# Four tokens per partition for the later query loads, one activation table set for Ln and Exp, and new instruction orders, in a fused linear-attention and feed-forward kernel

## The chip, the cores and the metric

The kernel runs on one core of a Trainium2 chip. The metric is the device time of one execution in microseconds, as the median of several runs. A core has five engines with a queue each: TensorE (PE, with its weight loads as PEld), VectorE (DVE), ScalarE (ACT), GpSimd (POOL) and SyncE (SP), which here only issues transfers. Sixteen DMA engines move the data.

## The reference

Two functions run one after the other: a decaying linear attention and a feed-forward layer with a sine.

```python
def _attn_ref(q, k, v, lam):            # q, k, v: (4, 8, 768, 64)
    pos = np.arange(64); rel = pos[:, None] - pos[None, :]
    Dmask = np.where(rel >= 0, lam[:, None, None] ** rel, 0.0)
    for b in range(12):
        sl = slice(64 * b, 64 * b + 64)
        qb, kb, vb = q[:, :, sl], k[:, :, sl], v[:, :, sl]
        intra = (qb kb^T * Dmask) vb
        out[:, :, sl] = intra + (qb * lam ** (pos + 1)) kv_state
        kv_state = lam ** 64 * kv_state + (kb * lam ** (63 - pos))^T vb

def _moe_ref(x, w_in, w_out, alpha):    # x: (3072, 512), d_ff = 2048
    h = x @ w_in
    s = np.sin(alpha * h)
    g = h + s * s / (alpha + 1e-9)
    return g @ w_out
```

The products above are written in words; `x` is the attention's output with the eight heads side by side. Inputs and output are 32-bit floats.

## The kernel before

**Tiling.** Attention works on 24 blocks of 128 tokens, six for each of the four batch entries (`NB` = 6). Instead of a decay mask, query and key are scaled by powers of lambda (tables `Lq`, `Lk`, `Lp`, `Lq4`, made from `exp(n ln lambda)` in the prologue), so that a 0/1 mask is left. For each block, `scale_block` multiplies the loaded 32-bit `q32` and `k32` by their table into the bf16 tile `qk2` and casts `v32` into `v2`. `piece_Q`, `piece_K` and `piece_T` transpose `qk2` into `qkT`, on TensorE for the first eight blocks, by a transposing transfer issued from SP for the rest. `part_S` makes the score products, which VectorE multiplies by the mask into `Sm` (L629); `part_O` adds the masked scores times `v2` and the queries times the running state; `part_Z` accumulates the state in one bank, from which `Zd` or `Zc` is evicted. The attention result of a block is evicted transposed into `xT` (L732, and L745 for the first four blocks).

**Feed-forward.** Six chunks of 512 tokens. `unit_A` and `unit_A2` (L828, L862) multiply `w1` by `xT`; ScalarE takes the sine (`t16`), ScalarE or POOL squares it (`u16`), VectorE adds it to the product as `gT` (L845, L880), which frees the bank. `unit_B` (L893) is the second product for chunk 0. From chunk 1 on the second product is done with seven half-size products instead of eight (`unit_P`, L981): `weight_sums` (L936) and `token_sums` (L959) form the sums that this needs, and `finish` combines the seven terms through `kept` (L1018, L1021, L1027) before the stores. `store` (L913) puts the stores of chunk 0 on ScalarE's queue.

**Order.** Every operation is recorded by `_Plan.op` with what it reads and writes. The order on each engine, and for operations that several engines can do also the engine, is written out by hand as lists of operation numbers in `_Plan.ORDER` (L38 to L103). `_settle` walks these lists; `emit` puts a semaphore wait before each operation whose input comes from elsewhere. Each queue runs strictly in its list's order. A pair `(n, cols)` in TensorE's list is a filler: n products of `cols` columns on constant data, which keep TensorE busy in the prologue.

**The prologue.** The loads of the first four blocks go out on SP, 3 MB in runs of 1,024 bytes (`load_q(0)`: four tokens of a head in each partition). ScalarE takes `Ln` of lambda (L438), then a first `Exp` (L440, a table load), VectorE multiplies by the exponents (`lnL`, L441), ScalarE takes the four tables (L443 to L449) and loads the table for the sine (L450). Then come scalings, transposes, scores and masks for four blocks, and the first unit of the feed-forward (L862).

**The later query loads.** For each pair of blocks s, s + 1 from 4 on, `load_q` issues one load of 512 KB: partition p holds tokens 2p and 2p + 1 of all eight heads, in runs of 512 bytes. So the queries of a pair come out of the transposes split by token parity, and `queries(s)` gives for a block two runs of 64 columns, one of each parity. Scores and results then have their 128 query columns in the order (parity, index); the mask of these blocks (`mask[2]`) is made for it, and the eviction to `xT` puts them back in order, writing every second bf16 element.

## Time and profile before

| | us |
|---|---|
| three runs | 210.6, 210.4, 210.04 |
| median | 210.4 |
| the profiled execution | 209.95 |
| its span, first to last instruction | 208.2 |
| mean granted TensorE clock | 1.000 |

A row of the timeline is start, length, engine, line, operation, output and inputs, and in brackets the idle time before it with what ended it. A row of the groups is line, engine, operation, names, shapes and count, then the busy time in all and the mean in ns of one, then the idle time before. Rows of the waits are total, times, longest. `PEld` overlaps `PE`. `SPq`, `ACTq` and `POOLq` are the engines' own queues while they issue a transfer. The span also shows 34.40 MB moved at 165 GB/s on average, 83,222 packets, 59,632 of them under 512 bytes.

### The profile page before, as it was taken

Reading aid. Unit: us, or ns where it says so; the run is one execution under the profiler, and the core shown is the slowest. Engines: PE = TensorE matmul, PEld = TensorE weight load, DVE = VectorE, ACT = ScalarE, POOL = GpSimd, SP = SyncE. Lnnn points to the kernel's source line nnn. Section 1 sums busy time; section 2 is a strip of 40 time slices with the busy share of each in tenths; the row PEclk is TensorE's granted clock in tenths of the full one; section 3 lists DMA queues with packets and bytes.
Section 4 is the critical chain, followed back from the end, with each engine's and each line's share of the span. In section 5 each row is a group of like instructions: output and inputs, shape, how many; then the busy total and the mean of one; then the engine's idle time right before and its main releaser. Section 6 shows DMA issues by size and latency. Waiting matters only on the chain.

```text
span 208.2 us, 4897 instructions
## 1 busy us (share of the span) xinstructions
PE 200.0 (96%) x1972; PEld 136.8 (66%) x1972; DVE 168.5 (81%) x296; ACT 147.7 (71%) x270; POOL 132.4 (64%) x140
## 2 busy tenths in 40 slices
PE   6988999999997999998999999999999999999995
PEld 6756444557765877665657576665667666667994
DVE  2898567886989999987988979899798866767854
ACT  5658999448998999976979776898765579734300
POOL 6065689834968987954796850958851695585400
DMA  4999999999899999799997999380300004000324
GB/s 133 323 315 216 202 255 214 213 238 245 197 179 230 232 250 248 154 215 206 208 245 156 242 271 185 67 194 26 136 0 3 0 32 169 3 0 20 128 94 165
DMA packets 83222, 34.40 MB, mean 165 GB/s; under 512 B 59632, under 2 KB 80384, under 8 KB 83200
## 3 DMA queue, kind: packets, MB, share of 16 engines
q1 hardware_dynamic: 78544, 29.24, 62.5%
q0 software_dynamic: 3696, 3.67, 10.9%
q10 hardware_dynamic: 960, 1.19, 1.9%
q8 instruction: 15, 0.25, 0.5%
q14 instruction: 7, 0.06, 0.1%
HBM read 27.28 MB, written 6.29 MB: 161 GB/s over the span
## 4 chain that ended last, share of the span: by engine, by line
PE 79%; DVE 9%; ACT 4%; DMA 3%; SPq 2%; issue 1%; ACTq 1%; POOL 0%
PE bank L828 28%; PE bank L981 26%; PE bank L862 7%; PE bank L893 6%; PE bank L722 3%; PE bank L618 3%; DMA v<-in_v_dram 3%; SPq L324 2%; DVE gT L880 2%; DVE Sm L629 2%; DVE gT L845 2%; PE bank L700 1%; DVE w L936 1%; PE bank L654 1%; ACT Zd L672 1%; PE bank L662 1%
## 5 line engine op out<-in xcount | busy, mean ns | idle before, releaser
L828 PE MATMUL bank<-xT,w 128*128 128x512 bf16 x296 | 70.9, 380 | 1.0 <-ACT kept L1018 0.7
L845 DVE SCALAR_TENSOR_TENSOR gT<-u,rinv,bank 128x512 bf16<-128x512 bf16 x74 | 53.6, 744 | 18.2 <-ACT u L842 14.1
L838 ACT ACTIVATE t<-bank,alpha 128x512 bf16<-128x512 f32 x74 | 49.9, 683 | 19.9 <-PE bank L828 19.0
L828 PEld LDWEIGHTS bank<-xT,w 128*128 128x128 bf16 x296 | 27.8, 98 | 28.8 <-DVE gT L845 1.4
L959 POOL TENSOR_TENSOR gT<-gT 128x512 bf16<-128x512 bf16 x28 | 32.1, 1158 | 14.1 <-DVE Xs L959 8.9
L842 ACT ACTIVATE u<-t 128x512 bf16<-128x512 bf16 x57 | 35.2, 628 | 1.5
L843 POOL TENSOR_TENSOR u<-t 128x512 bf16<-128x512 bf16 x17 | 17.6, 1040 | 25.7 <-ACT t L838 25.7
L629 DVE TENSOR_TENSOR Sm<-bank,mask 128x1024 bf16<-128x1024 f32 x24 | 28.9, 1216 | 3.0 <-PE bank L618 1.1
L862 PE MATMUL bank<-xT,w 128*128 128x256 bf16 x176 | 21.6, 273 | 1.0 <-DVE gT L880 1.0
L880 DVE SCALAR_TENSOR_TENSOR gT<-u,rinv,bank 128x256 bf16<-128x256 bf16 x44 | 18.9, 474 | 4.2 <-ACT u L876 3.5
L959 POOL TENSOR_TENSOR Xs<-gT 128x512 bf16<-128x512 bf16 x19 | 21.8, 1162 | 0.3 <-DVE gT L845 0.3
L981 PE MATMUL bank<-w,gT 128*128 128x256 bf16 (+1 forms) x168 | 20.1, 268 | 0.0
L872 ACT ACTIVATE t<-bank,alpha 128x256 bf16<-128x256 f32 x44 | 18.5, 471 | 2.0 <-PE bank L862 1.7
L981 PE MATMUL bank<-ws,gT 128*128 128x256 bf16 x160 | 19.6, 273 | 0.0
L981 PE MATMUL bank<-w,Xs 128*128 128x256 bf16 (+1 forms) x168 | 19.5, 268 | 0.0
L478 POOL TENSOR_TENSOR qk<-q,Lq 128x512 bf16<-128x512 f32 x17 | 18.2, 1077 | 2.0 <-DMA q<-in_q_dram 2.0
L497 POOL TENSOR_TENSOR qk<-k,Lk 128x512 bf16<-128x512 f32 x16 | 17.4, 1090 | 3.3 <-DMA k<-in_k_dram 3.2
L862 PEld LDWEIGHTS bank<-xT,w 128*128 128x128 bf16 x176 | 16.3, 98 | 4.2 <-DVE gT L880 1.8
L981 PEld LDWEIGHTS bank<-w,gT 128*128 128x128 bf16 x168 | 15.9, 98 | 4.1 <-DVE gT L959 0.2
L981 PEld LDWEIGHTS bank<-w,Xs 128*128 128x128 bf16 x168 | 15.6, 98 | 3.3
L981 PEld LDWEIGHTS bank<-ws,gT 128*128 128x128 bf16 x160 | 15.3, 98 | 3.1 <-ACT xT L732 0.4
L893 PE MATMUL bank<-w,gT 128*128 128x512 bf16 x64 | 15.8, 380 | 0.0
(105 smaller groups left out, 266.0 us busy)
## 6 DMA issues: line engine op xcount, KB each, us to landing
k<-in_k_dram SPq DMA_DIRECT2D x24, 256.0 KB, 5.1
q<-in_q_dram SPq DMA_DIRECT2D x12, 512.0 KB, 6.2
v<-in_v_dram SPq DMA_DIRECT2D x24, 256.0 KB, 5.8
out_dram<-osb SPq DMA_DIRECT2D x18, 256.0 KB, 2.6
w<-in_moe_w_out_dram POOLq DMA_DIRECT2D x4, 512.0 KB, 7.8
w<-in_moe_w_in_dram POOLq DMA_DIRECT2D x3, 512.0 KB, 8.1
ws<-in_moe_w_in_dram SPq DMA_DIRECT2D x2, 512.0 KB, 7.5
out_dram<-osb ACTq DMA_DIRECT2D x8, 128.0 KB, 3.7
```

The costliest lines, as they stand in the source:

```text
L478: lambda e, a=a: e.tensor_tensor(qk2[:, j:j + 2, 4 * a:4 * a + 4, :], q32[:, jq, 4 * a:4 * a + 4, :, :].rearrange("p h t d -> p t h d"), b ...
L629: op("DVE", lambda e: e.tensor_tensor(Sm[js][:, :, :], banks[:, 512 * b0:512 * b0 + 1024].rearrange("p (c i) -> p c i", i=128), bass.AP(ma ...
L828: ins = e.matmul(ps[hb][:, c0:c1], w1[:, kc, 128 * m:128 * (m + 1)], xT[x][:, kc, c0:c1], start=(kc == 0 and c0 == lo), stop=(kc == NKC - ...
L838: op("ACT", lambda e: e.activation(t16[ju][:, w], ps[hb][:, w], ACTF.Sin, scale=alpha[:, m:m + 1]), 0.69 if hi - lo == TCH else 0.475, [ba ...
L842: lambda e: (e.activation(u16[ju][:, w], t16[ju][:, w], ACTF.Square) if e is nc.scalar else e.tensor_tensor(u16[ju][:, w], t16[ju][:, w], ...
L845: op("DVE", lambda e: e.scalar_tensor_tensor(out=gT[g][:, m, w], in0=u16[ju][:, w], scalar=rinv[:, m:m + 1], in1=ps[hb][:, w], op0=ALU.mul ...
L862: ins = e.matmul(ps[hb][:, 256 * i:256 * i + 256], w1[:, kc, 128 * (m + i):128 * (m + i + 1)], xT[x][:, kc, lo:lo + 256], start=(kc == 0 a ...
L872: op("ACT", lambda e, i=i: e.activation(t16[ju][:, 256 * i:256 * i + 256], ps[hb][:, 256 * i:256 * i + 256], ACTF.Sin, scale=alpha[:, m + ...
L880: op("DVE", lambda e, i=i: e.scalar_tensor_tensor(out=gT[g][:, m + i, lo:lo + 256], in0=u16[ju][:, 256 * i:256 * i + 256], scalar=rinv[:, ...
L893: ins = e.matmul(ps[ob][:, w], gT[g][:, m, 128 * s4:128 * (s4 + 1)], w2[:, m, w], start=(m == 0), stop=(m == NM - 1),)
L959: e.tensor_tensor(dst, in0, in1, alu), 0, rd, wr))
L981: ins = e.matmul(ps[ob][:, lo + d0:lo + d1], lhs, rhs[:, d0:d1], start=first and p == 0, stop=(p == NM // 2 - 1), skip_group_check=True)
```

## The change

Four things change together.

1. The query load of a pair of blocks from 4 on becomes two loads of 256 KB. Half x of the partitions (0 to 63, 64 to 127) takes heads 4x to 4x + 3; partition p of a half holds the four tokens 4p to 4p + 3 of each of its heads, so runs are 1,024 bytes. Accordingly the tables `Lq` are made anew for such partitions, the scaling writes two of the four token positions for each of two `qk2` tiles, `queries` gives four runs of 32 columns, the mask is made for four tokens, and the eviction writes every fourth bf16 element of `xT`.
2. One table set that holds both logarithm and exponential is loaded on ScalarE right behind the load of `alpha`, by an explicit instruction.
3. The index tables are split: `E_i` gets the parts for keys and for the first blocks, and a part for the later queries that two iotas on POOL make, one for each half of the partitions, with a cast of its own and two products `lnLq` on VectorE.
4. The first two weight sums are declared to overwrite the whole of `ws`; and all five lists of `ORDER` are new. There are 1,065 operations instead of 1,050: ten query loads, two iotas, a cast and two products more.

In the new lists TensorE begins with 55 + 43 fillers of 128 columns (64 before); SP issues both first query loads ahead of the first keys; ScalarE's tables come in the order `Lk`, `Lp`, `Lq4`, `Lq`; VectorE takes the first `lnLq`, a mask memset and the cast of the identity ahead of `lnL`. ScalarE holds 288 operations instead of 278, VectorE 297 instead of 296, POOL 130 instead of 136, SP 111 instead of 101. By kind: 18 of the 20 evictions L732 are on ScalarE instead of 12, 80 squares instead of 76, and 3 evictions of `kept` (L1018, whole or half) fewer; of the ten weight sums POOL has four instead of three, the first half of term 7 among them.

```diff
         "PE": (
-            (64, 128), 58, (5, 512), 60, 54, (11, 128), 38, 56, 52, 61, 66, 64, (1, 128), 68, 69, 74, 77,
+            (55, 128), (43, 128), 43, 59, 63, 61, 65, 57, 66, (2, 128), (1, 512), 69, 73, 74, 71, (3, 512), 77,
...
         "ACT": (
-            1, 30, 31, 34, 36, 35, 33, 37, 59, 39, 57, 53, 71, 70, 76, 75, 82, 50, 83, 97, 87, 88, 94, 98, 125,
+            1, 33, 34, 38, 37, 36, 41, 42, 44, 60, 62, 67, 76, 75, 80, 81, 56, 88, 102, 93, 99, 98, 139, 133,
...
         "DVE": (
-            20, 16, 17, 32, 23, 44, 19, 43, 42, 45, 41, 40, 48, 26, 55, 63, 62, 67, 65, 78, 73, 85, 80, 91, 93,
+            19, 20, 23, 39, 26, 22, 35, 40, 48, 47, 46, 45, 49, 50, 64, 58, 29, 68, 54, 70, 72, 78, 83, 87, 90,
...
-                last["q32", s] = load(
-                    q32[:, j, :, :, :].rearrange("p h t d -> p h (t d)"),
-                    q[b, :, n * BL:(n + 2) * BL, :].rearrange("h (p t) d -> p h (t d)", t=2),
-                    [("q32", j, 0), ("q32", j, 1)], 2.0, f"q32{j}", lat=2.7, after=after, runs=64,
-                )
+                for x in range(2):
+                    last["q32", s] = load(
+                        q32[64 * x:64 * x + 64, j, :, :, :].rearrange("p (h y) t d -> p h (y t d)", y=2),
+                        q[b, 4 * x:4 * x + 4, n * BL:(n + 2) * BL, :].rearrange("h (p t) d -> p h (t d)", t=4),
+                        ("q32", j, x), 1.42, f"q32{j}" + "h" * x, lat=2.7, after=after, runs=16,
+                    )
...
-            load(alphaT[:, :], bass.AP(moe_alpha.tensor, 0, [[128, NM], [1, 128]]), "alphaT", 0.1, "alphaT", "ACT", lat=2.0, runs=1)
+            def load_alpha(e):
+                ins = e.dma_start(alphaT[:, :], bass.AP(moe_alpha.tensor, 0, [[128, NM], [1, 128]]))
+                e.preload_act_table_set("natural_log_exp_and_others")
+                return ins
+
+            op("ACT", load_alpha, 0.1, dma="alphaT", lat=2.0, issue=0.55, runs=1, writes=["alphaT"])
...
+            for r in ((0, 64), (64, 128)):
+                part = op("POOL", lambda e, r=r: e.iota(E_i[r[0]:r[1], ne:], [[256, NB // 2], [1, 4]], base=0,
+                                                        channel_multiplier=4), 0.3, writes=[("E_q", r[0])])
+                part.some = True
+            op("POOL", lambda e: e.tensor_copy(E_f[:, ne:], E_i[:, ne:]), 0.1, [("E_q", 0), ("E_q", 64)], ["E_qf"])
...
-                t, ks = (4, 2) if i < 2 else (2, 1)
+                t, ks = 4, 2 if i < 2 else 1
...
+            for x in range(2):
+                r = slice(64 * x, 64 * x + 64)
+                op("DVE", lambda e, r=r, x=x: e.tensor_tensor(
+                    lnLq[r, :, :], bass.AP(E_f, 64 * x * (ne + 2 * NB) + ne, [[ne + 2 * NB, 64], [1, 2 * NB], [0, 4]]),
+                    bass.AP(lnlam, 64 * x * H + 4 * x, [[H, 64], [0, 2 * NB], [1, 4]]), ALU.mult), 0.2,
+                   ["E_qf", "lnlam"], [("lnLq", x)])
+            op("ACT", lambda e: e.activation(Lq[:, :, :], lnLq[:, :, :], ACTF.Exp), 0.2,
+               [("lnLq", 0), ("lnLq", 1), "warm"], ["Lq"])
...
-                           qk2[:, j:j + 2, 4 * a:4 * a + 4, :],
-                           q32[:, jq, 4 * a:4 * a + 4, :, :].rearrange("p h t d -> p t h d"),
-                           bass.AP(Lq, n * H + 4 * a, [[(NB + 4) * H, 128], [H, 2], [1, 4], [0, D]]), ALU.mult),
-                       1.05, [("q32", jq, a), "Lq"], [("q2", j, a), ("q2", j + 1, a)]))
+                           qk2[:, j + a, 0:H, :].rearrange("p (t h) d -> p t h d", t=2),
+                           bass.AP(q32, jq * H * 2 * D + 2 * a * D, [[RL * H * D, 128], [D, 2], [4 * D, 4], [1, D]]),
+                           bass.AP(Lq, (n // 2 * 4 + 2 * a) * 4, [[8 * NB, 128], [4, 2], [1, 4], [0, D]]), ALU.mult),
+                       1.05, [("q32", jq, 0), ("q32", jq, 1), "Lq"], [("q2", j + a, 0), ("q2", j + a, 1)]))
...
+            def queries(s, r, jp):
+
+                if s < 4:
+                    return qkT[r, 0:4, jp, 32 * s:32 * s + 32]
+                jq, u = s % RT // 2 * 2, 64 * (jp // 2) + 32 * (s % 2)
+                return qkT[r, jq:jq + 2, 0:4, u:u + 32].rearrange("p a (b h) x -> p h a b x", h=2)[:, jp % 2]
...
+            def in_order(dst, s):
+                return dst.rearrange("p a (u x t) -> p a u t x", u=2, t=2) if s < 4 else dst.rearrange("p a (x t) -> p a t x", t=4)
...
-                        wr = [("T", i, x) for x in m] + ([("ws", 256 * (i // 3))] if i < 4 else [] if i == 4 else keys)
+                        wr = [("T", i, x) for x in m] + ([("ws", 0), ("ws", 256)] if i < 4 else [] if i == 4 else keys)
```

More of the change, by code (lines that the diff above doesn't have):

```diff
@@ L295, in bass_lightning_attn__then__act_snake_kernel @@
         lnlam = sb("lnlam", [128, H], F32)
-        E_i = sb("E_i", [128, 2 * NB + 4, H], I32)
-        E_f = sb("E_f", [128, 2 * NB + 4, H], F32)
-        lnL = sb("lnL", [128, 2 * NB + 4, H], F32)
-        Lq = sb("Lq", [128, NB + 4, H], F32)
+        E_i = sb("E_i", [128, (NB + NP + 4) * H + 2 * NB], I32)
+        E_f = sb("E_f", [128, (NB + NP + 4) * H + 2 * NB], F32)
+        lnL = sb("lnL", [128, NB + NP + 4, H], F32)
+        lnLq = sb("lnLq", [128, 2 * NB, 4], F32)
+        Lq = sb("Lq", [128, 2 * NB, 4], F32)
+        Lq4 = sb("Lq4", [128, 4, H], F32)
         Lk = sb("Lk", [128, NB, H], F32)
@@ L632, in then @@
                         bass.AP(mask[mi], 0, [[128, 128], [0, 8], [1, 128]]), ALU.mult), 1.19 if s < NP else 1.22, [bank(b0), bank(b1), ("mask", mi)], [("Sm", js)])
-                return mm, 0.2 if s < NP else 0.33, [("qT", jq + t, a) for t in range(nq) for a in range(2)] + [("kT", jt)], [bank(b0), bank(b1)], then
+                return mm, 0.2 if s < NP else 0.33, query_keys(s) + [("kT", jt)], [bank(b0), bank(b1)], then
             def diag(s):
@@ L690, in part_O @@
                 sm = [s // 2 * 2 % 4 + t for t in range(2)] if s < NP else [s % 2]
-                reads = [("v2",) + y for y in of_block(s)] + [("Sm", i) for i in sm] + [("qT", jq + t, a) for t in range(nq) for a in range(2)]
+                reads = [("v2",) + y for y in of_block(s)] + [("Sm", i) for i in sm] + query_keys(s)
                 wide = n and diag(s - 1)
@@ L790, in mm @@
                     return ins
-                op("PE", mm, 0.34, [("qT", jq + t, a) for t in range(nq) for a in range(2)] +
+                op("PE", mm, 0.34, query_keys(s) +
                    [("Zd", (s - 1) % 2, 0), ("Zd", (s - 1) % 2, 1)], [bank(b) for b in obs])
```

73 lines of the change are left out of this document (38 added, 35 removed), and 104 rows, old and new, of the table ORDER.

## The prediction

> **What bounds the kernel now.** I read the page first: engine totals, then the chain of waits by line.
>
> ```profile
> span 208.2 us, 4897 instructions
> PE 200.0 (96%) x1972; PEld 136.8 (66%) x1972; DVE 168.5 (81%) x296; ACT 147.7 (71%) x270; POOL 132.4 (64%) x140
> PE 79%; DVE 9%; ACT 4%; DMA 3%; SPq 2%; issue 1%; ACTq 1%; POOL 0%
> ```
>
> TensorE is busy 96% of the span, and 79% of the chain lies on it. What can still be gained is therefore its idle time, so I cut the span into stretches. The columns are length; busy time of PE, PEld, DVE, ACT and POOL with counts; granted clock; DMA share; GB/s.
>
> ```profile
> 0.00:19.04 19.04, 15.55 (x280) 12.66 (x281) 13.28 (x24) 11.75 (x24) 8.66 (x22) 1.00 0.96 251
> 19.04:58.00 38.96, 38.95 (x313) 22.40 (x312) 29.47 (x49) 30.50 (x58) 28.59 (x29) 1.00 1.13 223
> 58.00:100.00 42.00, 40.01 (x443) 28.58 (x442) 39.15 (x73) 36.25 (x73) 30.33 (x29) 1.00 1.11 211
> 100.00:205.60 105.60, 105.52 (x944) 73.13 (x942) 86.34 (x151) 69.25 (x117) 64.81 (x61) 1.00 0.45 111
> 205.60:208.20 2.60, 0.00 (x0) 0.00 (x0) 0.29 (x1) 0.00 (x0) 0.00 (x0) 1.00 0.46 149
> ```
>
> From 19.04 us, where the first product with `w1` starts, TensorE idles 0.01 us up to 58, 2.0 us between 58 and 100, and 0.1 us from there to 205.60; the last 2.6 us are the last eviction and store. Only the prologue and the middle stretch can give anything, and in the middle VectorE has just 42.00 - 39.15 = 2.85 us free and ScalarE 5.75. TensorE's own waits name the two places:
>
> ```profile
> PE bank L862 <- DVE gT L880: 1.0, 1, 1.0
> PE bank L828 <- ACT kept L1018: 0.7, 1, 0.7
> ```
>
> No wait of TensorE there ends on a transfer.
>
> **The change, part by part: the prologue.** The timeline of its path:
>
> ```profile
> 3.59 0.29 POOL L418 CAST E_f<-E_i 128x128 f32<-128x128 int32 x1
> 3.86 0.21 ACT L438 ACTIVATE lnlam<-lam_bc 128x8 f32<-128x8 f32 x1 [1.33 <-DMA lam_bc<-in_lam_dram]
> 4.09 1.28 ACT L440 ACT_TABLE_LOAD   x1
> 4.11 0.29 DVE L441 TENSOR_TENSOR lnL<-E_f,lnlam 128x128 f32<-128x128 f32 x1 [2.36 <-ACT lnlam L438]
> 5.95 0.69 DVE L485 TENSOR_TENSOR qk<-k,Lp 128x512 bf16<-128x512 f32 x1 [1.41 <-ACT Lp L445]
> 5.95 0.23 ACT L447 ACTIVATE Lk<-lnL 128x48 f32<-128x48 f32 x1
> 6.09 0.21 ACT L443 ACTIVATE Lq<-lnL 128x32 f32<-128x32 f32 x1
> 8.80 1.29 DVE L468 TENSOR_TENSOR qk<-q,Lq 128x512 bf16<-128x512 f32 x2 [0.21 <-DMA q<-in_q_dram]
> ...
> 12.18 4.62 DVE L629 TENSOR_TENSOR Sm<-bank,mask 128x1024 bf16<-128x1024 f32 x4 [0.37 <-PE bank L618]
> 16.72 1.34 DVE L745 CAST xT<-bank 128x512 bf16<-128x512 f32 x2
> 18.00 0.76 ACT L672 CAST Zd<-bank 64x256 bf16<-64x256 f32 x2
> 19.04 0.38 PE L862 MATMUL bank<-xT,w 128*128 128x256 bf16 x2
> ```
>
> With one set for both functions the load at 4.09 goes: 1.28 us off the way from lambda to the first decay table. [...] But what follows was not waiting for that load alone. In the new lists POOL makes two more index tables and one more cast around `E_f`; each is smaller than that cast (0.29), some 0.2 us, and the last ends near 4.4 instead of 3.88. VectorE puts the first new product `lnLq`, which waits for it, and two small operations ahead of `lnL`, which so ends at about 5.3 instead of 4.40. The three exponentials follow 0.14 us apart (5.95 and 6.09 above), and the one that the queries need is third: near 5.85. The first scaling starts at 5.9 where it started at 5.95, so the saved load is spent. Behind it the four query scalings and the two first key scalings, six of some 0.67 us, end at 5.9 + 4.0 = 9.9; now the same six end at 8.80 + 1.29 = 10.09. The warm-up products, 98 short ones in a row, end before that.
>
> The score products then reach VectorE 0.2 us earlier: the four mask products (4.62) would end at 16.6, now 16.80. There the new list gives VectorE two half evictions of the state, `Zd` (0.42 us each, row below), which ScalarE does now, between the four mask products and the eviction of block 0: 16.6 + 0.42 + 0.67 + 0.42 + 0.67 = 18.8. ScalarE saves 0.38 of the 0.76 at 18.00, so its own end moves from 18.76 to some 18.2. Behind the later of the two the first unit starts within 0.3 us, as it does now (18.76 to 19.04): 18.8 to 19.1 against 19.04. I take 0 for the prologue. Ends: -0.7, if VectorE's small operations fit into waits that I counted as work, and +0.7, if the second evictions meet the `w1` cast that ScalarE still does ahead of its half.
>
> **The middle stretch.** Here are the two stalls, first that of 0.97 us:
>
> ```profile
> 62.24 2.13 DVE L936 TENSOR_TENSOR w<-w 128x1024 bf16<-128x1024 bf16 x2
> 65.21 1.05 PE L862 MATMUL bank<-xT,w 128*128 128x256 bf16 x8 [0.97 <-DVE gT L880]
> ```
>
> Two sums of the second weight stand in a row on VectorE ahead of the `gT` pair that frees the bank. In the new list one of them (term 7, first half) is POOL's, and the other stands elsewhere, with three units and a block's attention products in hand on TensorE. So this stall goes: -0.97. The second:
>
> ```profile
> 93.77 1.66 ACTq L913 DMA_DIRECT2D out_dram<-osb  x2
> 95.49 0.59 ACTq L913 DMA_DIRECT2D out_dram<-osb  x1
> 97.44 0.59 ACT L1018 COPY kept<-bank 128x512 f32<-128x512 f32 x1
> 98.08 1.04 PE L828 MATMUL bank<-xT,w 128*128 128x512 bf16 x4 [0.73 <-ACT kept L1018]
> ```
>
> ScalarE issues three stores (1.66 + 0.59 = 2.25 us of its time) in the 4 us before it copies the bank that TensorE needs. In the new list that copy stands ahead of the last two stores of this chunk and the others come earlier: -0.73. What the rest of the new lists costs cannot be read from this trace. It lies between nothing and the 2.0 us that the present lists lose in the same stretch, and with VectorE at 93% I take +0.5. What moves between the engines is near a balance: four `xT` evictions go from VectorE to ScalarE, about as much goes from ScalarE to VectorE and POOL.
>
> **The evictions.** For blocks 4 to 23 neighbouring results now land 8 bytes apart in `xT`, not 4.
>
> ```profile
> L732 ACT CAST xT<-bank 128x512 bf16<-128x512 f32 x12 | 8.8, 737 | 2.5 <-PE bank L662 1.5 <-PE bank L722 0.9
> L1018 ACT COPY kept<-bank 128x512 f32<-128x512 f32 x6 | 3.5, 584 | 5.4 <-PE bank L981 5.4
> L1018 ACT COPY kept<-bank 128x256 f32<-128x256 f32 x2 | 0.7, 372 | 0.9 <-PE bank L981 0.9
> L672 DVE CAST Zd<-bank 64x256 bf16<-64x256 f32 x10 | 4.2, 420 | 1.0 <-PE bank L662 0.9
> L618 PE MATMUL bank<-qkT 64*128 64x128 bf16 x160 | 8.0, 219 | 0.1
> L618 PE MATMUL bank<-qkT 64*64 64x128 bf16 x64 | 1.5, 220 | 0.7 <-ACT qkT L544 0.7
> ```
>
> A copy of as many values without steps takes ScalarE 584 ns, the 4-byte step 737: a surcharge of 153. At 8 bytes the further cost lies between 0 and 271: if the step halves the rate, the part that grows with the length, 2 x (584 - 372) = 424, comes twice, 584 + 424 = 1,008 in all. I take 0, nearest to the row of the same shape. [...] TensorE now reads queries in four runs of 32 columns instead of two of 64; the second score row has four runs already, and costs 220 against 219: 0. Scalings, transposes and masks keep their counts and shapes: 0.
>
> **The loads.** POOL's waits for them:
>
> ```profile
> POOL v L500 <- DMA v<-in_v_dram: 4.9, 2, 2.9
> POOL qk L478 <- DMA q<-in_q_dram: 2.0, 2, 1.3
> ```
>
> Ten loads of 512 KB in runs of 512 bytes become twenty of 256 KB in runs of 1,024. The runs of 1,024 bytes and more in the prologue move 251 GB/s over the whole stretch, later ones 211: at those rates 5.2 MB take 21 us of the engines instead of 25. Ten more issues stand in SP's queue, before key and value loads and the transposes. Behind them wait POOL's casts and scalings, which already lose 4.9 and 2.0 us on loads without TensorE waiting for them; that slack is the cover. If it were gone, ten issues of some 0.6 us, as ScalarE's above, are spread over 110 us: about half a microsecond for the block that is late. I take 0; ends -0.3 and +0.5.
>
> **Sum**, against the profiled execution's 209.95 us (span 208.2 and 1.75 around it): 209.95 - 0.97 - 0.73 + 0.5 = 208.75. The median of the runs is 0.45 above the profiled one, so 209.2 us.
>
> **The rivals.**
>
> *Everything pays.* The prologue keeps 0.7 us and no new stall replaces the old two: 210.4 - 1.7 - 0.7 = 208.0. For it: both stalls have an edit that meets them. Against: the spent table load above. Chance 0.08.
>
> *The stalls only move.* The lists lose in other places what they gain in these two: 210.4. One such place can be read: in the new POOL list the first weight sum stands ahead of block 4's key scaling, which now comes first.
>
> ```profile
> 32.00 1.05 POOL L478 TENSOR_TENSOR qk<-q,Lq 128x512 bf16<-128x512 f32 x1
> 35.82 1.05 POOL L497 TENSOR_TENSOR qk<-k,Lk 128x512 bf16<-128x512 f32 x1
> 36.83 4.20 POOL L936 TENSOR_TENSOR ws<-w 128x1024 bf16<-128x1024 bf16 x2
> 38.48 0.39 PE L516 MATMUL bank<-ident,qk 128*128 128x128 bf16 x4
> ```
>
> Two query scalings in a row from 32.0 end at 34.1, sum and key scaling at 34.1 + 2.1 + 1.05 = 37.3. The reader is the transpose at 38.48: 1.2 us in hand. The new list also issues one more 512 KB of `w2` before these queries; at 223 GB/s that is 2.4 us, and 2.4 - 1.2 = 1.2 us would be lost. To this case belongs that the preloaded set does not serve, and a second load is put in again: the first unit starts 1.2 us later and eats most of the 1.7. Chance 0.20.
>
> *Stepped evictions make ScalarE the bound between 58 and 100 us: slower.* Some nine `xT` evictions fall to ScalarE there by the new list. At 1,008 ns instead of 737 that is 9 x 0.27 = 2.4 us, each ahead of the activation that frees the next bank: 209.2 + 2.4 = 211.6. It outweighs the gain from 0.13 us per eviction. For it: a 4-byte step already costs 153 ns; against: 5.75 us of free time on ScalarE there. Chance 0.27.
>
> **How the numbers follow.** My forecast, 208.4 to 209.7, has 0.45. About 0.3% (0.63 us) is what a measurement of this kernel can tell from no change. Faster: 0.45 + 0.08 less the edge, 0.51. Same: 0.20. Slower: 0.27 and the edges, 0.29. The range reaches from just under "everything pays" to the slower rival: 207.9 to 211.9; the forecast's own is 208.4 to 209.7.
>
> **What would show it.** Right: two table loads instead of three, the first `w1` product within 0.7 us of 19.04, no idle over 0.5 us on TensorE from 58 to 100 us, `xT` evictions at 737 ns, and DMA time that changes without moving the span. Wrong: a first `w1` product before 18.3 (the table load was worth its 1.28), `xT` above 870 ns with TensorE waiting for ScalarE, or TensorE waiting for transposes or key scalings near 40 us.

## The result: 221.2 us, and the profile after

The changed kernel takes 221.19 us (median of six runs, 219.93 to 221.92) where the kernel before takes 210.36 in the same setting (six runs, 209.94 to 211.46): 1.0502 times as long, 95% interval 1.0461 to 1.0544. The prediction said 209.2, in 207.9 to 211.9; the time lies far outside. The profiled execution took 221.63 us. First its page: span, busy times, chain of waits by engine and by line.

```profile
span 219.9 us, 4969 instructions
PE 203.7 (93%) x1993; PEld 137.6 (63%) x1993; DVE 168.2 (77%) x297; ACT 160.1 (73%) x279; POOL 125.7 (57%) x134
PE 56%; ACT 18%; DMA 14%; SPq 4%; DVE 4%; issue 1%; POOL 1%; ACTq 0%
```

TensorE's share of the chain falls from 79% to 56%; ScalarE has 18% of it instead of 4, transfers 14 instead of 3. The same stretches as in the prediction (length; busy PE, PEld, DVE, ACT, POOL with counts; clock; DMA share; GB/s) say where:

```profile
0.00:19.04 19.04, 15.86 (x293) 12.98 (x293) 13.72 (x27) 9.83 (x21) 10.12 (x27) 1.00 0.90 237
19.04:58.00 38.96, 34.60 (x232) 18.13 (x233) 25.26 (x37) 25.93 (x48) 19.18 (x18) 0.96 1.14 207
58.00:100.00 42.00, 38.85 (x452) 28.21 (x451) 37.84 (x74) 39.40 (x77) 31.10 (x30) 1.00 1.15 214
100.00:215.00 115.00, 112.61 (x1002) 76.80 (x1000) 90.13 (x158) 84.96 (x136) 65.26 (x61) 1.00 0.45 105
```

From 19.04 to 58 us TensorE now idles 38.96 - 34.60 = 4.36 us (0.01 before) and its granted clock falls to 0.96. From 58 to 100 it idles 3.15 (2.0 before) while ScalarE's busy time grows from 36.25 to 39.40; behind 100 us 2.4 (0.1 before). In the whole span the idle time grows from 208.2 - 200.0 = 8.2 to 219.9 - 203.7 = 16.2; the other 3.7 us of the longer span are longer busy time, part of it at the lower clock. TensorE's waits by name (in all, times, longest):

```profile
PE bank L540 <- POOL qk L521: 3.2, 1, 3.2
PE bank L865 <- ACT xT L774: 1.8, 5, 0.5
PE bank L1177 <- DVE Xs L436: 1.5, 1, 1.5
PE bank L865 <- DVE gT L882: 1.2, 2, 0.9
PE bank L899 <- DVE gT L917: 0.7, 1, 0.7
PE bank L899 <- ACT xT L774: 0.6, 2, 0.4
PE bank L755 <- ACT xT L774: 0.6, 1, 0.6
```

The wait for `kept` of 0.73 us is gone. For `gT`, where there was one wait of 0.97, the rows show three, of 1.2 and 0.7 us in all. New are a transposition that waits 3.2 us for the key scaling of block 4, and 3.0 us of waits for `xT`. The first has a chain of its own, here from the chain in order of time (start, length, what):

```profile
16.58 8.78 DMA w<-in_moe_w_in_dram
...
26.78 14.78 DMA k<-in_k_dram
41.56 0.07 issue
41.62 1.05 POOL qk L521
42.68 0.14 issue
42.81 0.58 PE bank L540 x4
```

The keys of block 4 are issued at 26.78 us and land 14.78 us later. POOL's first weight sum, which the prediction had put in their way, was done by 38.55 us. The wait costs more than its length: from 42 to 45 us TensorE's clock is 0.57. Two short stretches, and the timeline's rows of the same eight products just behind the wait and 3.7 us later:

```profile
42.00:45.00 3.00, 2.19 (x9) 1.10 (x10) 2.35 (x1) 0.59 (x1) 3.00 (x3) 0.57 0.86 196
45.00:47.00 2.00, 2.00 (x18) 0.90 (x17) 1.23 (x3) 0.00 (x0) 2.00 (x3) 0.79 1.21 243
```

```profile
43.19 3.20 PE L930 MATMUL bank<-w,gT 128*128 128x512 bf16 x8
...
46.89 1.89 PE L930 MATMUL bank<-w,gT 128*128 128x512 bf16 x8
```

At a clock of 0.57 they take 3.20 us instead of 1.89, so the wait of 3.2 loses some 4.5 in this execution.

It is not the same in every execution. The mean clock of the six was 0.992 four times, 0.998 and 1.000, and the one at 1.000 took 221.47 us all the same. Two kernels below differ from the change only in the evictions of block 4 and later, the first of which runs at 50 us; their profiles show waits for these keys of 2.1 us (evictions turned round) and, without steps, of only

```profile
PE bank L540 <- POOL qk L521: 0.5, 1, 0.5
```

The waits for `xT` come from its eviction (groups; before: 737 and 735 ns):

```profile
L774 ACT CAST xT<-bank 128x512 bf16<-128x512 f32 x18 | 23.5, 1305 | 3.8 <-PE bank L697 1.8 <-PE bank L705 1.5 <-PE bank L764 0.3
L774 DVE CAST xT<-bank 128x512 bf16<-128x512 f32 x2 | 2.6, 1305 | 0.0
```

The prologue, last: the first `w1` product starts at 19.59 us instead of 19.04, behind two table loads instead of three.

### The profile page after: what moved, and what is told of

Read it like the earlier page. It is cut to its first block, busy times and chain, and to the rows that moved or that the text cites. A ratio compares the mean times of both kernels' runs of the same rounds, so it can differ in the third digit from the quotient of the medians.

```text
span 219.9 us, 4969 instructions
## 1 busy us (share of the span) xinstructions
PE 203.7 (93%) x1993; PEld 137.6 (63%) x1993; DVE 168.2 (77%) x297; ACT 160.1 (73%) x279; POOL 125.7 (57%) x134
## 4 chain that ended last, share of the span: by engine, by line
PE 56%; ACT 18%; DMA 14%; SPq 4%; DVE 4%; issue 1%; POOL 1%; ACTq 0%
PE bank L1018 24%; PE bank L865 20%; ACT xT L774 7%; DMA k<-in_k_dram 7%; SPq L328 4%; DMA w<-in_moe_w_in_dram 4%; ACT t L909 4%; PE bank L899 3%; DMA v<-in_v_dram 3%; PE bank L930 3%; ACT u L913 3%; ACT t L875 2%; PE bank L661 2%; PE bank L764 1%; ACT u L879 1%
## 5 line engine op out<-in xcount | busy, mean ns | idle before, releaser
L865 PE MATMUL bank<-xT,w 128*128 128x512 bf16 x296 | 72.4, 380 | 2.9 <-ACT xT L774 1.8
L882 DVE SCALAR_TENSOR_TENSOR gT<-u,rinv,bank 128x512 bf16<-128x512 bf16 x74 | 54.2, 744 | 24.9 <-ACT u L879 20.6
L865 PEld LDWEIGHTS bank<-xT,w 128*128 128x128 bf16 x296 | 27.2, 98 | 30.6 <-ACT xT L774 3.3
L879 ACT ACTIVATE u<-t 128x512 bf16<-128x512 bf16 x62 | 39.0, 633 | 2.0 <-DVE gT L882 0.4
L996 POOL TENSOR_TENSOR gT<-gT 128x512 bf16<-128x512 bf16 x27 | 30.7, 1155 | 9.2 <-DVE gT L882 2.8
L880 POOL TENSOR_TENSOR u<-t 128x512 bf16<-128x512 bf16 x12 | 12.5, 1044 | 29.3 <-ACT t L875 29.3
L774 ACT CAST xT<-bank 128x512 bf16<-128x512 f32 x18 | 23.5, 1305 | 3.8 <-PE bank L697 1.8
L996 POOL TENSOR_TENSOR Xs<-gT 128x512 bf16<-128x512 bf16 x17 | 19.5, 1156 | 6.6 <-DVE gT L882 6.6
L521 POOL TENSOR_TENSOR qk<-k,Lk 128x512 bf16<-128x512 f32 x18 | 18.7, 1043 | 5.4 <-DMA k<-in_k_dram 5.4
L1018 PE MATMUL bank<-ws,gT 128*128 128x256 bf16 x160 | 19.9, 273 | 0.6 <-DVE Xs L996 0.5
L1018 PE MATMUL bank<-w,gT 128*128 128x256 bf16 (+1 forms) x168 | 20.4, 268 | 0.0
L1018 PE MATMUL bank<-w,Xs 128*128 128x256 bf16 (+1 forms) x168 | 19.8, 268 | 0.0
L899 PEld LDWEIGHTS bank<-xT,w 128*128 128x128 bf16 x176 | 16.3, 98 | 5.3 <-ACT xT L774 1.8
L1018 PEld LDWEIGHTS bank<-w,gT 128*128 128x128 bf16 x168 | 15.7, 98 | 4.3 <-POOL gT L996 0.3
L1018 PEld LDWEIGHTS bank<-w,Xs 128*128 128x128 bf16 x168 | 15.7, 98 | 4.1 <-DVE osb L1064 0.3
L1018 PEld LDWEIGHTS bank<-ws,gT 128*128 128x128 bf16 x160 | 15.4, 98 | 4.5 <-DVE Xs L996 0.9
L502 POOL TENSOR_TENSOR qk<-q,Lq 128x512 bf16<-128x512 f32 x16 | 16.5, 1043 | 2.7 <-DMA q<-in_q_dram 2.6
```

Of the source, the lines that this page charges most:

```text
L521: lambda e: e.tensor_tensor(qk2[:, j, H:2 * H, :], block32(k32, jl), lk, ALU.mult), 1.05,
L774: op(eng, lambda e, a0=a0, a1=a1: (e.copy if e is nc.scalar else e.tensor_copy)(in_order(xT[c % RX][:, a0:a1, BL * i4:BL * (i4 + 1)], s), ...
L865: ins = e.matmul(ps[hb][:, c0:c1], w1[:, kc, 128 * m:128 * (m + 1)], xT[x][:, kc, c0:c1], start=(kc == 0 and c0 == lo), stop=(kc == NKC - ...
L879: lambda e: (e.activation(u16[ju][:, w], t16[ju][:, w], ACTF.Square) if e is nc.scalar else e.tensor_tensor(u16[ju][:, w], t16[ju][:, w], ...
L882: op("DVE", lambda e: e.scalar_tensor_tensor(out=gT[g][:, m, w], in0=u16[ju][:, w], scalar=rinv[:, m:m + 1], in1=ps[hb][:, w], op0=ALU.mul ...
L899: ins = e.matmul(ps[hb][:, 256 * i:256 * i + 256], w1[:, kc, 128 * (m + i):128 * (m + i + 1)], xT[x][:, kc, lo:lo + 256], start=(kc == 0 a ...
```

## The experiments

All ratios are to the kernel before, run beside each kernel, with their 95% interval. The kernel before took 210.27 to 210.71 us beside all of them, so that times of different experiments can be subtracted to within some 0.4 us.

### The layout and the lists apart

The five lists can be carried over to the other layout, since the operations are the same but for the ten split loads and five small prologue operations. So the change was taken apart: lists without layout, layout without lists, and both with evictions that do not step.

**The lists alone.**

```diff
 # the kernel before; the change's lists in its numbers, e.g. TensorE's
-            (64, 128), 58, (5, 512), 60, 54, (11, 128), 38, 56, 52, 61, 66, 64, ...
+            (55, 128), (43, 128), 38, 54, 58, 56, 60, 52, 61, (2, 128), (1, 512), ...
```

> The kernel before (its query layout, its tables, its 4-byte steps) with the five lists of the changed kernel; the two half loads of a pair of query blocks are again one load, at the place of the first half. Theory A (two causes: the late load of block 4's keys, which the lists cause, is worth some 6 us, the 8-byte steps some 4, the prologue 0.6): 216 to 218.5 us, with TensorE waiting some 3 us for a key scaling near 42 us. Theory B (the stepped evictions are the whole of it): 209.5 to 211.5. Theory C (the lists are the whole of it, steps cost nothing on the path): 220 to 222.

Measured: 216.02 us, ratio 1.0301 (1.0236 to 1.0366). TensorE waits 2.1 us for block 4's keys and 1.1 for its queries, which is all that it idles more than before between 19.04 and 58 us (3.18 against 0.01).

```profile
PE bank L514 <- POOL qk L495: 2.1, 1, 2.1
PE bank L537 <- POOL qk L476: 1.1, 2, 0.5
```

Between 58 and 100 us it idles 1.84 us, where the old lists lose 2.0: the two stalls that the lists remove there come back as others, 1.1 us for a transposing transfer and 0.7 for `gT`. Behind 100 us it idles 0.9 instead of 0.1, and 4.1 us pass behind its last product instead of 2.6.

```profile
58.00:100.00 42.00, 40.16 (x478) 29.84 (x476) 39.74 (x78) 37.91 (x77) 29.82 (x28) 1.00 1.11 223
```

**The layout alone.**

```diff
 # the changed kernel; the lists of before in its numbers, e.g. TensorE's
-            (55, 128), (43, 128), 43, 59, 63, 61, 65, 57, 66, (2, 128), (1, 512), ...
+            (64, 128), 63, (5, 512), 65, 59, (11, 128), 43, 61, 57, 66, 71, 69, ...
```

> The changed kernel (its query layout, its tables, its 8-byte steps) with the five lists of the kernel before; the two half loads stand next to each other where the one load stood. Theory A: no stall near 42 us; xT evictions at some 1,300 ns, twelve on ScalarE and eight on VectorE as before, cost 2 to 5 us: 212 to 215.5. Theory B: 219 to 222. Theory C: 209.5 to 211.

Measured: 216.05, ratio 1.0276 (1.0242 to 1.031); no wait for keys near 42 us.

**The same without steps.**

```diff
 def in_order(dst, s):
-    return (...) if s < 4 else dst.rearrange("p a (x t) -> p a t x", t=4)
+    return (...) if s < 4 else dst
 def by_token(src, s, n):
-    return (...) if s < 4 else src.rearrange("p (a t x) -> p a t x", a=n, t=4)
+    return (...) if s < 4 else src.rearrange("p (a x) -> p a x", a=n)
```

> As the layout alone, but the evictions of blocks 4 to 23 write xT without steps, so that the rows of these blocks come out in another order within each 128. Theories A and B: evictions at 584 ns, the time goes back to 209 to 210.8. Theory C: the same as with steps, within 0.5 us.

> The changed kernel with its own lists, but the evictions of blocks 4 to 23 write xT without steps, so that the rows of these blocks come out in another order within each 128. Theory A: the stall near 42 us stays, the waits for xT go: 216.5 to 218.5. Theory B: 209.5 to 211.5. Theory C: 220 to 222.

Measured: the layout with old lists 213.23, 1.0129 (1.0083 to 1.0176), with evictions at 584 ns:

```profile
L772 ACT CAST xT<-bank 128x512 bf16<-128x512 f32 x12 | 7.0, 584 | 2.5 <-PE bank L703 1.5 <-PE bank L762 0.9
```

The change with its own lists, also without steps, took 217.20, 1.0329 (1.0304 to 1.0353), evictions at 582. So the steps are worth 216.05 - 213.23 = 2.8 us with the old lists and 221.19 - 217.20 = 4.0 with the new. Theories B and C fall. A holds for the lists alone (216.02 at the edge of its 216 to 218.5) and for the time without steps, but not for the stall that it expected to stay there (0.5 us in the profile). And it falls for the layout: 216.05 lies above its 215.5, and without steps the layout is not back at 210, it keeps 2.9 us that none of the three theories had.

### What else the layout costs: issues or partitions

```diff
 # the kernel before, load_q from block 4 on
-    last["q32", s] = load(q32[:, j].rearrange("p h t d -> p h (t d)"),
-        q[b, :, n * BL:(n + 2) * BL].rearrange("h (p t) d -> p h (t d)", t=2), ...)
+    for x in range(2):                                   # halves by heads
+        last["q32", s] = load(q32[:, j, 4 * x:4 * x + 4].rearrange(...),
+            q[b, 4 * x:4 * x + 4, n * BL:(n + 2) * BL].rearrange(...), ...)
+    for x in range(2):                                   # or halves by partitions
+        last["q32", s] = load(q32[64 * x:64 * x + 64, j].rearrange(...),
+            q[b, :, (n + x) * BL:(n + x + 1) * BL].rearrange(...), ...)
```

> The kernel before, each later load of a pair's queries (512 KB) issued as two of 256 KB, one for each group of four heads over all 128 partitions; nothing else differs. Theory D (the number of issues in SP's queue is what the new layout loses 2.9 us by): 212 to 214. Theory E (it is the load into 64 partitions): 210 to 210.8. Theory G (neither, the prologue's small operations): 210 to 210.8.

> The kernel before, each later load of a pair's queries issued as two of 256 KB into 64 partitions each (first the even block, then the odd one), runs of 512 bytes as before. Theory D: 212 to 214, the same as with halves by heads. Theory E: 212 to 214 here alone. Theory G: 210 to 210.8 in both.

Measured: halves by heads 210.21, ratio 1.0012 (0.998 to 1.0043); halves by partitions 213.54, 1.0166 (1.0116 to 1.0216). The same ten issues more, the same bytes, the same runs of 512 bytes: only the loads into 64 partitions cost, 3.2 us. (A scaling must wait for both of these halves, but in the kernel before it waits for the whole load too, without loss.) Theory E holds. The stretch from 20 to 60 us, first of the halves by heads, then by partitions:

```profile
20.00:60.00 40.00, 39.99 (x330) 23.15 (x328) 29.74 (x50) 31.76 (x61) 29.29 (x30) 1.00 1.17 222
```

```profile
20.00:60.00 40.00, 37.65 (x294) 21.36 (x291) 28.94 (x47) 29.33 (x56) 26.06 (x27) 1.00 1.13 204
```

The engines that transfer are nearly as busy (1.17 and 1.13) and move 204 GB/s instead of 222. That is no lack of demand: SP's queue moves 4.88 MB in 63.6% of the engines' time instead of 5.66 in 67.8%, some 8% less for the same share, and POOL's as much as before for its share (3.21 MB in 48.8%, 3.13 in 48.3). The value loads behind land late: POOL's wait for them grows from 4.9 to 5.6 us, its longest from 3.2 to 5.1, and TensorE idles 2.35 us in this stretch instead of 0.01, behind POOL's casts of these values (1.84 and 0.51).

```profile
POOL v L501 <- DMA v<-in_v_dram: 5.6, 3, 5.1
PE bank L701 <- POOL v L501: 1.8, 1, 1.8
```

Why loads into 64 partitions lower the rate is not shown.

### The steps of the evictions

**Turned round.** The same values, read with steps and written in rising order.

```diff
 # the changed kernel, s >= 4 (the kernel before alike with t=2)
-    dst.rearrange("p a (x t) -> p a t x", t=4)       <- src "p (a t x) -> p a t x"
+    dst.rearrange("p a (x t) -> p a x t", t=4)       <- src "p (a t x) -> p a x t"
```

> The changed kernel, its evictions of blocks 4 to 23 turned round: they write xT in rising order, one value behind the other, and step through the bank (every 32nd of its 4-byte values). Theory L (the cost lies in writes that are 8 bytes apart): evictions near 584 to 740 ns, 216.5 to 218, as without steps. Theory M (steps cost on either side): 1,000 ns or more, 219.5 to 222.

> The kernel before, its 20 evictions of blocks 4 to 23 turned round: they write xT in rising order and step through the bank (every 64th of its values). If a step on the reading side costs nothing, as the changed kernel with turned evictions shows, ScalarE's take 581 instead of 737 ns. If ScalarE's and VectorE's time between 58 and 100 us is on the path: 209.0 to 210.0. If not: 210.1 to 210.7.

Measured: the change with turned evictions 215.63, 1.0221 (1.017 to 1.0273); they take 581 ns.

```profile
L775 ACT CAST xT<-bank 128x512 bf16<-128x512 f32 x18 | 10.5, 581 | 4.2 <-PE bank L698 1.9 <-PE bank L706 1.7 <-PE bank L765 0.5
```

Steps through the bank cost nothing (581 ns; 582 without any step), steps in the writes everything (1,305): theory L. The time is 0.9 us better than L's 216.5 to 218. That recovers 5.6 us of the 10.8, with the rows of the output in their old order. Why it is 1.6 us more than leaving the steps out recovered, with evictions of the same length, is not shown. In the kernel before the turned eviction changes nothing: 210.13, 0.9998 (0.9973 to 1.0022). The 4-byte surcharge of 153 ns lies off the path.

**Wider steps.**

```diff
 # the kernel before
+    def step(s): return (4, 8, 16, 32, 2)[s // 4 - 1]      # in 2-byte values
-    dst.rearrange("p a (x t) -> p a t x", t=2)
+    dst.rearrange("p a (x t) -> p a t x", t=step(s))
```

> The kernel before, its evictions writing with steps of 8 bytes in blocks 4 to 7, 16 in 8 to 11, 32 in 12 to 15, 64 in 16 to 19 and 4 in 20 to 23, so that rows come out in another order within the blocks 4 to 19. If every value that starts a new 16-byte line costs, 8-byte steps take some 1,300 ns and wider ones twice that surcharge, above 2,000. If it is the step as such, all steps of 8 bytes and more take 1,300. The time itself: 212 to 222.

One run: 226.75 us. ScalarE's evictions in the timeline, one row for each step (8, 16, 32, 64, 4 bytes):

```profile
44.37 1.31 ACT L743 CAST xT<-bank 128x512 bf16<-128x512 f32 x1
...
69.18 2.47 ACT L743 CAST xT<-bank 128x512 bf16<-128x512 f32 x1
...
98.05 2.33 ACT L743 CAST xT<-bank 128x512 bf16<-128x512 f32 x1
...
135.35 2.43 ACT L743 CAST xT<-bank 128x512 bf16<-128x512 f32 x1 [1.71 <-PE bank L733]
...
165.36 0.74 ACT L743 CAST xT<-bank 128x512 bf16<-128x512 f32 x1 [0.84 <-PE bank L673]
```

The cost nearly doubles from 8 to 16 bytes (1.31 to 2.47 us) and grows no more with wider steps (2.33 and 2.43). With 160 ns that do not grow with the length (584 - 424, the prediction's rows), a value costs (2,440 - 160) / 512 = 4.45 ns at 16 bytes, 2.25 at 8 and 1.13 at 4. All five steps fit one price, an estimate from these rows: some 4.5 ns each time the eviction moves to another 16 bytes (four values there at 1.13 ns, two at 2.25 or one at 4.45). Written in rising order it would owe 0.56 ns a value by this estimate, less than the 0.83 (424 / 512) that it takes anyway. VectorE's evictions go the same way (1.31, then 2.31 to 2.43, then 0.73 us).

**The order put right in the stores**, in the hope of a faster kernel before:

```diff
 # the kernel before, evictions written without steps; stores of chunks 1 to 5
-    out[row:row + 128, lo:hi]
+    bass.AP(out.tensor, row * DM + lo, [[DM, 2], [2 * DM, 64], [1, hi - lo]])
```

> The kernel before, its 20 evictions of blocks 4 to 23 written without steps, and the order of the tokens put right in the stores of chunks 1 to 5 instead (row 2x+t from partition 64t+x, 2 KB or less a row as before). Theory H (what a step costs an eviction is worth something where ScalarE and VectorE are nearly full): evictions at 584 ns on ScalarE instead of 737, 209.0 to 210.0. Theory I (the surcharge of 4-byte steps lies off the path): 210.1 to 210.7.

Measured: 268.56, ratio 1.2741 (1.2684 to 1.2798). The evictions take 584 ns as meant, so neither theory was tested: the stores, whose rows are now named as two groups of 64 (every second row each), run at some 51 GB/s where nothing else runs, and the waits for them hold up the chain. The page's row of 40 slices, the last third of which holds hardly any transfers but stores, and the costliest of these waits:

```profile
GB/s 174 314 261 187 241 218 226 251 208 193 225 264 182 210 191 253 169 113 76 86 167 181 37 114 57 51 20 2 7 51 51 50 2 46 51 51 28 48 50 41
```

```profile
DVE osb L1035 <- DMA out_dram<-osb: 17.3, 4, 10.0
```

Where only stores run, the mean busy share of the 16 engines that transfer is 0.13, which is the work of two of them (16 x 0.13 = 2.1). No run tries another grouping of the rows.

```profile
234.00:238.00 4.00, 0.00 (x0) 0.00 (x0) 0.00 (x0) 0.00 (x0) 0.00 (x0) 0.50 0.13 50
```

### What the lists cost

**Block 4's loads in the changed kernel.** Operation 117 is the load of block 5's keys, 109 to 112 are w2's four parts, 202 and 203 the query scalings, 134 to 168 POOL's units.

```diff
 # SP, all three
-            100, 101, 114, 113, 115, 117, 116, 123, ...
+            100, 101, 117, 114, 113, 115, 116, 123, ...
 # POOL, keys first and w2 back
-            55, 107, 109, 108, 110, 134, 149, 111, 160, 168, 112, 164, 202, 203, ...
+            55, 107, 108, 134, 109, 149, 160, 110, 168, 111, 112, 164, 202, 203, ...
 # POOL, keys first and w2's later parts back
+            55, 107, 109, 108, 134, 149, 160, 168, 110, 164, 111, 202, 203, 112, ...
```

> The changed kernel, with one entry of SP's list moved: the load of block 5's keys stands ahead of block 4's queries again, so that it does not wait for w1's third part. Theory A1 (the block-4 loads are late because a load more stands behind that wait): the stall near 42 us shrinks from 3.2 us to under 1 us, 217 to 219. Theory A2 (they are late because 1 MB of w2 was issued before them): no change, 220 to 222.

> As the run with block 5's keys first, and the loads of the first three parts of w2 also go back behind the units that they followed in POOL's list of before. Theory A1: no further gain over that run, within 0.7 us. Theory A2: a further 2 to 4 us, 214 to 217. If both fall and the lists lose in other places, the time stays at 219 or more.

> The changed kernel, block 5's keys ahead of block 4's queries in SP's list, w2's first part issued as early as in the change, its second to fourth parts later (512 KB less ahead of block 4's keys). Theory A3 (it is a matter of bytes: the transfers run at their limit of some 210 GB/s, and the new lists ask for more of them by 42 us than it gives): k4 lands some 2 us earlier, its stall falls below 1.5 us, but half of the gain turns up as a wait for w2; 217.5 to 220. Theory A4 (a better list of loads does away with it): no wait over 0.7 us between 28 and 50 us, 215 to 217.

Measured: 219.86, 1.048 (1.0417 to 1.0543), the wait for the keys still 3.2 us; then 221.25, 1.0538 (1.0497 to 1.0579); then 219.73, 1.0453 (1.0395 to 1.0511). A1 and A4 fall. In their profiles the last two lose the wait for keys, and have these instead:

```profile
PE bank L928 <- DMA w<-in_moe_w_out_dram: 2.7, 1, 2.7
```

```profile
PE bank L928 <- DMA w<-in_moe_w_out_dram: 2.2, 1, 2.2
```

The wait moves from the keys to `w2` and hardly shrinks; A3 had its time (217.5 to 220) and the move, but expected half of the gain to stay. A2 expected a further 2 to 4 us from the second of the three, and there were none. In these two the key scaling starts at 38.95 and 39.31 us instead of 41.62; but without steps, with every load in its place, it started at 38.88, so these profiles alone don't show that moving the loads brings the keys earlier.

**The same places in the kernel before**, where nothing else differs (104 to 107 in its numbers are w2's four parts, 101 to 103 w1's).

```diff
 # the kernel before, POOL: two parts of w2 early
-            101, 102, 103, 198, 132, 104, 141, 148, 160, 164, 27, 105, 156, 106, 195, ..., 107, 196, ...
+            101, 102, 104, 103, 105, 198, 132, 141, 148, 160, 164, 27, 156, 106, 195, ..., 107, 196, ...
 # all four early
+            101, 102, 104, 103, 105, 198, 132, 141, 106, 148, 160, 107, 164, 27, 156, 195, ...
```

> The kernel before, with the loads of w2's first two parts issued as early in POOL's list as the change issues them (in the midst of w1's and right behind them); nothing else differs. Theory N (the places of the loads in the lists make block 4's keys late): 1 MB more ahead of them, k4 lands 2 to 5 us later than 35.8, TensorE waits 1 to 3 us at the transpose, 212 to 215. Theory O (the lists of the computing engines ask for the data too early; the loads' places are not the cause): 210 to 211.

> The kernel before, with all four loads of w2 as early in POOL's list as the change issues them: the first two in the midst of w1's, the third behind POOL's second unit, the fourth behind its fourth; nothing else differs. Theory P (the transfers run at their limit, and what is issued before and beside block 4's keys decides when they land): all 2 MB of w2 go out by 31.5 us instead of 35.8, k4's scaling starts at 39 to 41.5 instead of 35.82, TensorE waits 1.5 to 3.5 us for it, 212 to 215. Theory O (the lists of the computing engines are the cause): the scaling at 38 or before, 210 to 211.3.

Measured: 210.84, 1.0019 (0.9998 to 1.0039), and 213.17, 1.0122 (1.005 to 1.0194). With two parts early the key scaling starts at 37.56 instead of 35.82; with all four:

```profile
30.22 0.80 POOL L323 DMA_DIRECT2D w<-in_moe_w_out_dram  x1 [2.05 <-DMA w<-in_moe_w_in_dram]
31.04 1.05 POOL L842 TENSOR_TENSOR u<-t 128x512 bf16<-128x512 bf16 x1
32.13 1.41 DVE L844 SCALAR_TENSOR_TENSOR gT<-u,rinv,bank 128x512 bf16<-128x512 bf16 x2 [3.18 <-POOL u L842]
32.94 1.04 PE L827 MATMUL bank<-xT,w 128*128 128x512 bf16 x4 [1.84 <-DVE gT L844]
36.91 1.04 POOL L477 TENSOR_TENSOR qk<-q,Lq 128x512 bf16<-128x512 f32 x1 [3.57 <-DMA q<-in_q_dram]
40.92 1.04 POOL L496 TENSOR_TENSOR qk<-k,Lk 128x512 bf16<-128x512 f32 x1 [0.97 <-DMA k<-in_k_dram]
```

The keys' scaling is 5.1 us late by the places of `w2` alone, and the time grows by 2.5 us, both as theory P said. (With two parts N falls and O's time holds.) But TensorE does not wait for the keys here, against the expectation. It is late itself: the issue of `w2`'s fourth part stands in POOL's queue and must wait 2.05 us until a part of `w1` has landed, so the square behind it starts late (31.04), VectorE waits 3.18 us for it, and TensorE 1.84 for VectorE. Then it waits 0.56 for the queries. In the changed kernel the same issue holds POOL up for 1.94 us, but TensorE only for 0.24 behind it. So these 2.5 us can't be counted as a part of the 5.7 that the lists cost; they show that early `w2` makes the keys late, and a second way in which the place of a load can cost.

**SP's list exchanged alone**, either way.

```diff
 # the kernel before with the change's SP list in its numbers; and the lists alone with SP as before
-            0, 4, 3, 5, 2, 6, 7, 8, 9, 11, 10, 95, 96, 111, 108, 109, 110, 116, ...
+            0, 3, 2, 4, 5, 6, 7, 9, 8, 11, 10, 95, 96, 108, 109, 111, 110, 116, ...
```

> The kernel before with SP's list alone from the change (loads, DMA transposes and stores in the new order; a pair's queries are one load, at the place of the first half). Theory N: 211.5 to 215. Theory O: 210 to 211.

> The kernel before with the lists of TensorE, ScalarE, VectorE and POOL from the change, and SP's list as before. Theory N: at least 2 us of the 5.7 that all five lists cost come back, 212 to 214. Theory O: 215 to 217, the same as with all five.

Measured: 261.95 (1.2425, 1.2374 to 1.2475) and 246.60 (1.168, 1.1613 to 1.1747). Each list is tied to the others by its waits; half of a set says nothing of the whole, and these two tell nothing of N and O.

### The table set

```diff
 # the kernel before, with the load of alpha
+    e.preload_act_table_set("natural_log_exp_and_others")
```

> The kernel before, with the one table set for Ln and Exp asked for at the start, as the change does; its lists and everything else as before. Theory J (the prologue's path is set by the loads of q and v, so that the saved table load is worth nothing): two table loads, the first w1 product within 0.3 of 19.04 us, 210.0 to 210.7. Theory K (the load of 1.28 us lies on the path): first w1 product before 18.3, 209.0 to 209.6.

Measured: 210.16, 0.9984 (0.996 to 1.0009); first `w1` product at 19.40 us in its profile, 0.06 outside theory J's bound. Theory K falls; a gain below 0.4% can't be told from none. The first table is ready 1.24 us earlier (`Lp` starts at 4.44 instead of 5.68), and the scalings of the queries then wait for their loads, where the kernel before had 0.21 us of such waits:

```profile
6.47 1.29 DVE L473 TENSOR_TENSOR qk<-q,Lq 128x512 bf16<-128x512 f32 x2 [0.60 <-DMA q<-in_q_dram]
9.28 1.29 DVE L473 TENSOR_TENSOR qk<-q,Lq 128x512 bf16<-128x512 f32 x2 [0.91 <-DMA q<-in_q_dram]
```

## Why the prediction was wrong, step by step

**The evictions** ("I take 0", upper end 1,008 ns) failed by size. They take 1,305 ns, 568 more than before instead of 0 to 271. No run shows the 0 with which the sum was made, nor the halved rate on which the upper end rested. What the five steps fit is the estimated price per 16 bytes touched: two values in each cost 2.25 ns apiece, where values in rising order take 0.83. The rival "stepped evictions make ScalarE the bound" had the mechanism and 0.27 chance, but priced it with that end, and only between 58 and 100 us: nine evictions at 0.27, 2.4 us. There were six of them, at 0.57 us more each, and TensorE's waits for `xT` go on behind 100 us (0.5 at 115.69, 0.4 at 153.76 and at 174.83). Undoing the steps recovers 4.0 to 5.6.

**The loads** ("I take 0", -0.3 to +0.5) failed by their mechanism. The step priced ten more issues, which cost nothing (ratio 1.0012), and longer runs, with which the rate between 19.04 and 58 us fell (209 GB/s with the layout alone, 223 before); it did not ask which partitions a half load fills. That costs 2.9 us (layout without steps) to 3.2 (halves by partitions). The cover that it named, POOL's waits of 4.9 and 2.0 us, was the wrong sign to read: POOL, which waits for loads, is where the slower loads arrived first (4.9 us of waits for values became 5.6 with halves by partitions), and TensorE, with 0.01 us of idle time in that stretch, had nothing to give.

**The middle stretch** (-0.97 - 0.73 + 0.5): the two named stalls were read rightly, and the second is gone, but other stalls took back nearly all of the 1.2 us that the three terms promise: the lists alone idle 1.84 us there against 2.0.

**The lists ahead of it** are the third failure. The rival "the stalls only move" named the very place, more of `w2` ahead of block 4, and priced one part of 512 KB at 2.4 us less 1.2 in hand. All four parts had moved forward, and block 5's keys behind the wait for `w1`; the keys' scaling starts at 41.62 instead of 35.82. The transfers there run at 223 GB/s with the old lists and at 219 with the new ones alone, so what is asked for early makes something else late. In the profiled execution 3.2 us of waiting and 1.3 of slow clock stood there, in no term of the sum. That `w2` in its old places then comes too late by 2.2 to 2.7 us fits TensorE's new order, whose first product with `w2` starts at 28.20 us instead of 30.94. Of the lists' 5.7 us, the 3.2 of waits for block 4's keys and queries are located, and early `w2` is shown to make these keys late; which entries of the lists cost the rest stays open.

**The prologue** (0, ends -0.7 to +0.7) came out at +0.55 by its first product, inside its bounds, but partly by luck. The tables are as late as it worked out (the queries' at 5.77 us, forecast near 5.85). But the saved load is worth nothing (ratio 0.9984) even where no small operation stands in its way, since the queries' loads come next, and in the change too the first scaling waits for them until 6.23. VectorE's mask products end at 16.65, where 16.6 was forecast; then the path is another, for its first `Zd` waits for a product on values that landed late, in no step of the prediction:

```profile
13.55 0.61 POOL L515 CAST v<-v 128x512 bf16<-128x512 f32 x1 [1.98 <-DMA v<-in_v_dram]
17.18 0.42 DVE L715 CAST Zd<-bank 64x256 bf16<-64x256 f32 x1 [0.53 <-PE bank L697]
```

Of the signs that it named for being wrong, two came: `xT` above 870 ns with TensorE waiting for it, and TensorE waiting for a key scaling near 40 us.

The three causes overlap, since each delays the same work: lists 5.7, steps 2.8, partitions 2.9 with the old lists add up to 11.4, and the whole is 10.8. None of the versions beats the kernel before by more than the intervals allow for chance.

## What to carry to other kernels

Price a stepped write by the 16 bytes that it touches (here some 4.5 ns for each, an estimate), and let the step stand on the reading side of an eviction from a bank (581 ns here instead of 1,305). Keep a load on all 128 partitions where the transfers are as busy as here (222 GB/s between 20 and 60 us, 204 with 64 partitions); count the bytes that must land by each moment, not only the instructions, before moving a load forward (2 MB of `w2` asked for early made the keys' scaling 5.1 us late). A load's issue that must wait holds up the work behind it in the same queue (POOL's, for 2.05 us here). An engine with no idle time and its suppliers waiting for loads had no cover here: TensorE's 0.01 us of idle time became 2.35 with halves by partitions.

## What the runs showed of the hardware

- Evictions of 128x512 values from a bank, on ScalarE: 584 ns in rising order, 737 with 2-byte values 4 bytes apart, some 1,310 at 8, and 2,330 to 2,470 at 16, 32 and 64 bytes; 581 with the steps on the reading side.
- With the query loads of 256 KB into 64 partitions instead of 128 the core moved 204 GB/s instead of 222 between 20 and 60 us.
- A wait of TensorE of 2 to 3 us was in some cases followed by a lower clock: 0.57 from 42 to 45 us behind the wait of 3.2 here, 0.53 from 33 to 36 us behind that of 2.7 with the keys first and `w2` back, and 0.70 from 64 to 67 us behind one of 2.1 in the change without steps, but 1.00 from 42 to 45 us behind another of 2.1 with the lists alone (rows below, in this order). What decides whether the clock falls, and for how long, no run here shows.
- A store whose 128 rows are named as two groups of 64, every second row each, ran at some 51 GB/s, with the 16 engines that transfer busy 0.13 in mean.

The stretches behind the waits of 2.7, 2.1 and 2.1 us:

```profile
33.00:36.00 3.00, 3.00 (x9) 1.11 (x8) 0.94 (x2) 1.93 (x3) 2.04 (x2) 0.53 1.21 196
64.00:67.00 3.00, 3.00 (x25) 2.30 (x26) 2.42 (x3) 1.65 (x4) 1.03 (x3) 0.70 1.33 223
42.00:45.00 3.00, 2.71 (x25) 1.49 (x26) 2.96 (x2) 0.59 (x1) 3.00 (x3) 1.00 1.06 236
```
